# Whole float32 weights for the first two of twelve token blocks, and the second weight set decoded from block 5

## The chip, the cores and the metric

The kernel runs on one core of a Trainium2 chip. Its engines work side by side, each through its own queue in order: PE (TensorE, matrix products), DVE (VectorE), ACT (ScalarE), POOL (GpSimd) and SP, which here issues the DMAs. The metric is the time of one execution in microseconds; lower is better.

## The reference, cut to what matters

```python
# q, k, v, a_re, a_im: (4, 8, 768, 48); complex decay per step and channel, capped at 0.999
for t in range(S):
    S_re, S_im = a * S (complex product) + outer(k[t], v[t]) on the real part
    y[t] = q[t] @ S_re
x = y as (3072, 384)
gate = 1 / (1 + exp(-(x @ w_gate)))            # w_gate, w_val: 384 x 1536
x2 = (gate * (x @ w_val)) @ w_out              # w_out: 1536 x 384
h = x2 @ w_in                                  # 384 x 2048
out = (h - tanh(h)) @ w_out2                   # 2048 x 384
```

The kernel gets its weights as words of 64 bits (double precision) and makes float32 of them on the chip.

## The kernel before

The tokens are cut into 24 chunks of 128 for the recurrence ("attention") and into 12 blocks of 256 (two chunks) for the first feed-forward, called moe1. Its hidden width of 1536 is 12 slices f of 128 columns. For each block j and slice f there is one **step**, (j,f): `gv` forms the gate and value sums in PSUM from the block's x and the slice's two weight tiles; `gate` takes a tanh on ACT and forms g on DVE; `split` cuts g into a high part (ACT cast, float32r) and a low part (DVE subtraction); `outp`, three steps later (LAG1), adds g times the third weight tile to the block's output. The second feed-forward runs after all of this, in pieces of 512 tokens, on w2.

A product of float32 precision is made of three float32r products: high x high, high x low, low x high. So x, g and each weight exist as a pair of parts, and a gv step is 2 parts x 3 x 3 = 18 matmuls of 256 columns, an output step 9.

`Decoder` turns words into weights. A *tick* handles three words in three stages: `word_sign` on ACT (scaling, and the conversion of a byte), `word_value` on DVE (shift and or; with `direct` a second operation puts in the sign, otherwise ACT makes a sign tile with one more instruction and POOL multiplies by it), then `split`: an ACT cast into the high part and a POOL subtraction into the low part. `dec1` has the 36 tiles of moe1 (part 0 gate, 1 value, 2 output); seven words, listed in SIGNED, take the way with the sign tile. `dec2` has the 32 tiles of w2, all with the sign tile; they are spilled to DRAM (`w2d`) in blocks 2 to 10 and loaded back in block 11. `ring1` gives six raw buffers for the first 22 words and three for the others.

The order of steps is `order`: five steps of block 0, then steps of blocks 1 and 0 by turns, so that both use a slice soon after it is decoded, then the blocks 2 to 11 one after another. Attention for later chunks is set between the steps by due times. Within that, a scheduler fixes each engine's queue with its own estimates; SP's order is as written. PSUM holds two or three gv tiles, so a late gate holds up PE.

## Time and profile before

| | |
|---|---|
| three runs, median | 1139.35 us (1138.7 to 1139.69) |
| the profiled execution: time, span | 1139.4 us, 1137.6 us |
| PE, DVE, ACT, POOL busy, share of the span | 90%, 79%, 76%, 20% |
| gv matmuls (L735): count, busy | 2592, 348.2 us |
| output matmuls of moe1 (L769): count, busy | 1296, 187.2 us |
| matmuls of the second feed-forward (L898, L924), busy | 216.0 and 216.6 us |
| mean granted TensorE clock | 0.974 of 2.4 GHz |

A step of moe1 on blocks 2 to 11 shows as 18 + 9 matmuls and a few of attention between. The first feed-forward begins at about 79 us and ends at about 730. Busy times on PE overlap, since matmuls are pipelined: the pitch from one start to the next says more than a duration. The *gate* of a step is its DVE instruction L744 (g from th and gv).

### The profile page before, as it was taken

Reading aid. Unit: us, or ns where it says so; the run is one execution under the profiler, and the core shown is the slowest. Engines: PE = TensorE matmul, PEld = TensorE weight load, DVE = VectorE, ACT = ScalarE, POOL = GpSimd, SP = SyncE. Lnnn points to the kernel's source line nnn. Section 1 sums busy time; section 2 is a strip of 40 time slices with the busy share of each in tenths; the row PEclk is TensorE's granted clock in tenths of the full one; section 3 lists DMA queues with packets and bytes.
Section 4 is the critical chain, followed back from the end, with each engine's and each line's share of the span. In section 5 each row is a group of like instructions: output and inputs, shape, how many; then the busy total and the mean of one; then the engine's idle time right before and its main releaser. Section 6 shows DMA issues by size and latency. Waiting matters only on the chain.

```text
span 1137.6 us, 21667 instructions
## 1 busy us (share of the span) xinstructions
PE 1028.8 (90%) x8498; PEld 964.8 (85%) x8498; DVE 900.1 (79%) x1432; ACT 860.8 (76%) x1903; POOL 224.6 (20%) x182
## 2 busy tenths in 40 slices
PE   0348399999999999998999999999999999999996
PEld 0237399999999999988999999999989989999996
DVE  6999997879888988887978833487878778787875
ACT  8878796989888898877898783566767666676764
POOL 4554651131312232222323200000000000000000
PEclk9869799999999999999999999999999999999999
DMA  6223351223324424242333445700101010010000
GB/s 198 100 100 99 127 156 47 83 91 115 101 87 156 139 92 143 73 142 73 114 101 115 133 136 205 276 31 1 56 1 56 1 36 21 1 56 1 28 1 31
DMA packets 36400, 100.20 MB, mean 88 GB/s; under 512 B 4128, under 2 KB 7200, under 8 KB 36288
## 3 DMA queue, kind: packets, MB, share of 16 engines
q1 hardware_dynamic: 36288, 98.71, 26.4%
q8 instruction: 69, 1.13, 0.4%
q14 instruction: 43, 0.35, 0.1%
HBM read 76.68 MB, written 22.02 MB: 87 GB/s over the span
## 4 chain that ended last, share of the span: by engine, by line
PE 62%; DVE 14%; ACT 12%; issue 5%; DMA 3%; POOL 2%; SPq 0%; DVEq 0%; ACTq 0%; POOLq 0%
PE h L898 18%; PE o L924 17%; PE gv L735 14%; PE acc L769 7%; PE xps L604 2%; PE sc L569 2%; DMA raw<-in_w_dram 2%; DMA ri<-in_ri_dram 1%; ACT raw L68 1%; ACT raw L66 1%; DVE suf L519 1%; DVE sg L74 1%; PE gps L639 1%; POOL sg L84 1%; DVE B L532 1%
## 5 line engine op out<-in xcount | busy, mean ns | idle before, releaser
L735 PE MATMUL gv<-x,whl 128*128 128x256 f32 x2592 | 348.2, 289 | 29.6 <-DVE g L744 17.2
L735 PEld LDWEIGHTS gv<-x,whl 128*128 128x128 f32 x2592 | 327.5, 195 | 36.0 <-DVE g L744 18.3
L924 PE MATMUL o<-whl,gh 128*128 128x384 f32 x1152 | 216.6, 337 | 0.6 <-ACT gh L910 0.6
L898 PE MATMUL h<-x2h,whl 128*128 128x512 f32 x864 | 216.0, 394 | 0.0
L924 PEld LDWEIGHTS o<-whl,gh 128*128 128x128 f32 x1152 | 203.6, 188 | 9.3 <-ACT gh L910 0.9
L769 PE MATMUL acc<-gh,whl 128*128 128x256 f32 x1296 | 187.2, 288 | 3.1 <-ACT x L773 2.0
L898 PEld LDWEIGHTS h<-x2h,whl 128*128 128x128 f32 x864 | 160.9, 188 | 29.9
L769 PEld LDWEIGHTS acc<-gh,whl 128*128 128x128 f32 x1296 | 165.7, 191 | 7.8 <-ACT x L773 2.6
L91 ACT ACTIVATE s<-h 128x512 f32<-128x512 f32 x96 | 57.7, 601 | 111.3 <-PE h L898 111.3
L751 DVE TENSOR_TENSOR gh<-g,gh 128x256 fp32r<-128x256 f32 x144 | 76.6, 535 | 33.6 <-ACT gh L750 32.9
L911 DVE TENSOR_TENSOR gh<-g,gh 128x512 fp32r<-128x512 f32 x96 | 66.3, 690 | 42.0 <-ACT gh L910 41.3
L569 PE MATMUL sc<-qs,ks 112*128 112x128 f32 x384 | 56.7, 290 | 45.5 <-ACT qs L547 44.1
L99 DVE TENSOR_TENSOR th<-h,th 128x512 f32<-128x512 f32 x96 | 66.4, 692 | 31.5 <-ACT th L97 30.7
L569 PEld LDWEIGHTS sc<-qs,ks 112*128 112x128 f32 x384 | 51.3, 204 | 46.3 <-issue 34.2
L744 DVE SCALAR_TENSOR_TENSOR g<-th,gv 128x256 f32<-128x256 f32 x144 | 59.4, 413 | 36.7 <-ACT th L742 35.8
L750 ACT CAST gh<-g 128x256 fp32r<-128x256 f32 x144 | 57.8, 401 | 31.9 <-DVE g L744 31.3
L84 POOL TENSOR_TENSOR sg<-raw,sg 128x384 f32<-128x384 f32 x39 | 49.1, 1260 | 150.4 <-DVE raw L81 137.2
L100 DVE COPY_PREDICATED g<-mk,th 128x512 f32<-128x512 int32 x96 | 72.5, 755 | 1.0
L742 ACT ACTIVATE th<-gv 128x256 f32<-128x256 f32 x144 | 53.7, 374 | 25.6 <-PE gv L735 25.3
L910 ACT CAST gh<-g 128x512 fp32r<-128x512 f32 x96 | 59.3, 617 | 12.6 <-DVE g L100 12.3
L93 DVE SCALAR_TENSOR_TENSOR g<-g,s 128x512 f32<-128x512 f32 x96 | 65.5, 682 | 3.3 <-ACT g L92 3.3
L94 DVE TENSOR_TENSOR g<-g,h 128x512 f32<-128x512 f32 x96 | 65.0, 678 | 3.8 <-DVE g L93 0.9
(130 smaller groups left out, 1650.8 us busy)
## 6 DMA issues: line engine op xcount, KB each, us to landing
raw<-in_w_dram SPq DMA_DIRECT2D x68, 384.0 KB, 4.7
ri<-in_ri_dram SPq DMA_DIRECT2D x30, 448.0 KB, 4.3
w2d<-raw SPq DMA_DIRECT2D x32, 384.0 KB, 4.6
whl<-w2d SPq DMA_DIRECT2D x32, 384.0 KB, 5.0
qk<-in_qk_dram SPq DMA_DIRECT2D x24, 448.0 KB, 5.0
v<-in_vv_dram SPq DMA_DIRECT2D x24, 320.0 KB, 3.2
x2d<-x SPq DMA_DIRECT2D x12, 384.0 KB, 2.3
x2r<-x2d SPq DMA_DIRECT2D x12, 384.0 KB, 3.8
```

Source lines behind the costliest of these rows:

```text
L84: nc.gpsimd.tensor_tensor(w, raw[:, :, 0].bitcast(F32), sg, ALU.mult)
L93: nc.vector.scalar_tensor_tensor(g, g, TC * TB, s, ALU.add, ALU.mult)
L94: nc.vector.tensor_tensor(g, g, ps, ALU.mult)
L99: nc.vector.tensor_tensor(th, ps, th, ALU.subtract)
L100: nc.vector.copy_predicated(g, mk.bitcast(I32), th)
L569: nc.tensor.matmul(sc[:, i], ks[:, h // 2, h % 2], qs[:, h // 2, h % 2])
L735: nc.tensor.matmul(ps[:, part], w[:, wi, cs], x[:, xi, kt], start=(k == 0), stop=(k == 8))
L751: nc.vector.tensor_tensor(gh[:, 1], g, gh[:, 0].bitcast(F32), ALU.subtract)
L769: nc.tensor.matmul(o, w[:, wi, cs], gh[:, gi], start=(f == 0 and k == 0 and (m == 0 or m == 2 and not half)), stop=(f == NF1 - 1 and k == ...
L898: nc.tensor.matmul(ps.rearrange("p (z c) -> p z c", z=2), w[:, wi, cs], x[:, xi, :, kt], start=(k == 0), stop=(k == 8))
L911: nc.vector.tensor_tensor(gh[:, 1], g, gh[:, 0].bitcast(F32), ALU.subtract)
L924: nc.tensor.matmul(a[t], gh[:, gi, cs], w[:, wi], start=(f == 0 and k == 0), stop=(f == NF2 - 1 and k == 2), skip_group_check=True)
```

## The change

In blocks 0 and 1 (`WHOLE_GV`, `WHOLE_OUT`) the products are taken as single float32 matmuls of the whole weight, the whole x and the whole g. The decoder therefore keeps the whole float32 tiles (`F`) first; `part` makes the high and low parts of a tile later, on ACT and POOL: parts 0 and 1 of slice f after the gv step (1,f), part 2 after the output step (1,f). The whole tiles lie in slots that later hold other tiles' parts (`SLOT`, `whole_tile`), and all 36 words go through six raw buffers. For blocks 0 and 1 the low parts of x and g, and the cast of g, are gone. All words, those of w2 too, take the sign on DVE (`direct`): ACT has two instructions for a word in place of three, DVE two in place of one, POOL none in place of one. The w2 words are decoded in blocks 5 to 10 instead of 2 to 10.

```diff
-SIGNED = (6, 7, 8, 9, 10, 11, 16)
+WHOLE_GV, WHOLE_OUT = 2, 2
-SPILL_FROM, SPILL_TO = 2, 11
+SPILL_FROM, SPILL_TO = 5, 11
...
-            if 0 <= k - 2 < self.n:
+            if self.spill is not None and 0 <= k - 2 < self.n:
                 self.split(k - 2)
             if 0 <= k - 1 < self.n:
-                word_value(nc, self.raw[k - 1], self.sg[k - 1], self.sg[k - 1], self.direct(k - 1))
+                self.value(k - 1)
...
-                word_sign(nc, self.raw[k], self.sg[k], self.direct(k))
+                word_sign(nc, self.raw[k], None, True)
...
+        def value(self, s):
+            if self.spill is not None:
+                word_value(nc, self.raw[s], None, self.sg[s], True)
+                return
+            f, p = s // self.nparts, s % self.nparts
+            self.F[f, p] = whole_tile(f, p)
+            word_value(nc, self.raw[s], None, self.F[f, p], True)
+
+        def part(self, f, p):
+            w = self.F.pop((f, p))
+            hl = wp.tile([128, 2, 384], F32R, tag=f"w{SLOT[f, p]}", name="whl")
+            nc.scalar.copy(hl[:, 0], w)
+            self.low[(f * self.nparts + p) % len(self.low)].tensor_tensor(hl[:, 1], w, hl[:, 0].bitcast(F32), ALU.subtract)
+            self.W[f, p] = hl
...
+        SLOT[f, 2] = 30 + f if f < 6 else 12 + f
...
+        k, half = (24 + f, p) if p < 2 else (18 + f // 2, f % 2)
...
+            if j < WHOLE_GV:
+                nc.scalar.copy(hi.bitcast(F32), x)
+                return
...
-            w = dec1.W[f, part]
+            w = dec1.F[f, part] if j < WHOLE_GV else dec1.W[f, part]
...
+                if j < WHOLE_GV:
+                    nc.tensor.matmul(ps[:, part], w[:, cs], x[:, 0, kt].bitcast(F32),
+                                     start=(kt == 0), stop=(kt == 2))
+                    continue
...
+        if order[n][0] < WHOLE_OUT:
+            gtil[n] = m1g.tile([128, 2, N1], F32R, tag="gh", name="gh")
+            g = gtil[n][:, 0].bitcast(F32)
+            nc.vector.scalar_tensor_tensor(g, th, 1.0, ps[:, 1], ALU.add, ALU.mult)
+            return
...
+            if j < WHOLE_OUT:
+                nc.tensor.matmul(o, w[:, cs], gh[:, 0].bitcast(F32),
+                                 start=(f == 0 and (m == 0 or m == 2 and not half)),
+                                 stop=(f == NF1 - 1), skip_group_check=True)
+                continue
...
             gv(n)
+            if j == WHOLE_GV - 1:
+                dec1.part(f, 0)
+                dec1.part(f, 1)
...
                 outp(n - LAG1)
+                jo, fo = order[n - LAG1]
+                if jo == WHOLE_OUT - 1:
+                    dec1.part(fo, 2)
...
-        dec2 = Decoder(w2i, NF2, 2, ring0, lambda s: 2, (nc.gpsimd,), lambda s: False, w2d)
+        dec2 = Decoder(w2i, NF2, 2, ring0, lambda s: 2, (nc.gpsimd,), w2d)
```

The queues move with it. **PE**, among the alternating steps of blocks 1 and 0. Before, steps (1,4) and (0,9), then two output steps (x_835 is block 1's x, x_377 block 0's; the number behind x is a count of instructions):

```order
L735 MATMUL gv_1537<-x_835,whl_884 128x256 x9
L735 MATMUL gv_1537<-x_835,whl_977 128x256 x9
L735 MATMUL gv_1602<-x_377,whl_1487 128x256 x9
L735 MATMUL gv_1602<-x_377,whl_1572 128x256 x9
L769 MATMUL acc2_1298<-gh_1516,whl_874 128x256 x6
L769 MATMUL acc1_936<-gh_1516,whl_874 128x256 x3
L769 MATMUL acc0_935<-gh_1556,whl_1477 128x256 x6
L769 MATMUL acc1_936<-gh_1556,whl_1477 128x256 x3
```

After, steps (1,6) and (0,11) and two output steps (x_745 is block 1's x, x_358 block 0's; whole2 is a pair of whole tiles, and one row counts both parts):

```order
L763 MATMUL gv_1342<-x_745,whole2_981 128x256 x6
L763 MATMUL gv_1396<-x_358,whole2_1299 128x256 x6
L808 MATMUL acc2_1058<-gh_1287,whole2_854 128x256 x2
L808 MATMUL acc1_813<-gh_1287,whole2_854 128x256
L808 MATMUL acc0_812<-gh_1324,whole2_1294 128x256 x2
L808 MATMUL acc1_813<-gh_1324,whole2_1294 128x256
```

A gv step has 6 products for 18, an output step 3 for 9; a product counts once here.

**POOL**, around the work for chunk 4's ks and qs (L546 and L548 before, L571 and L573 after). Before (L84 is the sign multiplication, L312 a low part of a weight):

```order
L84 TENSOR_TENSOR sg_872<-raw_871,sg_872 128x384
L312 TENSOR_TENSOR whl_1153<-sg_882,whl_1153 128x384
L312 TENSOR_TENSOR whl_1146<-sg_872,whl_1146 128x384
L312 TENSOR_TENSOR whl_1160<-sg_892,whl_1160 128x384
L312 TENSOR_TENSOR whl_1244<-sg_985,whl_1244 128x384
L312 TENSOR_TENSOR whl_1254<-sg_996,whl_1254 128x384
L546 TENSOR_TENSOR ks_121<-qk_918,ri_703 112x4x128
L546 TENSOR_TENSOR qs_120<-qk_918,ri_703 112x4x128
L548 TENSOR_TENSOR qs_120<-qk_918,ri_703 48x4x128
L312 TENSOR_TENSOR whl_1264<-sg_1006,whl_1264 128x384
L312 TENSOR_TENSOR whl_1360<-sg_1252,whl_1360 128x384
```

After (L317 is a low part, L561 and L562 scale k and q):

```order
L561 TENSOR_TENSOR qk_626<-qk_626,suf_113 112x512
L562 TENSOR_TENSOR qk_626<-qk_626,B_631 112x512
L573 TENSOR_TENSOR ks_121<-qk_626,cosb_114 48x4x128
L571 TENSOR_TENSOR ks_121<-qk_626,ri_399 112x4x128
L571 TENSOR_TENSOR qs_120<-qk_626,ri_399 112x4x128
L577 TENSOR_TENSOR qs_120<-qk_626,cosb_114 48x4x128
L317 TENSOR_TENSOR whl_1276<-whole2_861,whl_1276 128x384
L571 TENSOR_TENSOR ks_121<-qk_795,ri_628 112x4x128
L571 TENSOR_TENSOR qs_120<-qk_795,ri_628 112x4x128
L573 TENSOR_TENSOR qs_120<-qk_795,ri_628 48x4x128
L317 TENSOR_TENSOR whl_1569<-whole2_1178,whl_1569 128x384
```

Five of the six weight instructions ahead of chunk 4's products have left that place; the low parts follow later in the queue.

**DVE**, ahead of the gate of step (1,0). Before (L74 and L77 are the two operations of a word, L744 a gate):

```order
L77 SCALAR_TENSOR_TENSOR sg_1006<-raw_1005,sg_1006 128x384
L74 SCALAR_TENSOR_TENSOR sg_1252<-raw_1251 128x384
L77 SCALAR_TENSOR_TENSOR sg_1252<-raw_1251,sg_1252 128x384
L74 SCALAR_TENSOR_TENSOR sg_1262<-raw_1261 128x384
L77 SCALAR_TENSOR_TENSOR sg_1262<-raw_1261,sg_1262 128x384
L463 TENSOR_TENSOR ri_920<-ri_920,carry_119 112x4
L464 SCALAR_TENSOR_TENSOR ri_920<-keep_110,ri_920 112x512
L548 TENSOR_TENSOR ks_121<-qk_918,ri_703 48x4x128
L74 SCALAR_TENSOR_TENSOR sg_1272<-raw_1271 128x384
L77 SCALAR_TENSOR_TENSOR sg_1272<-raw_1271,sg_1272 128x384
L744 SCALAR_TENSOR_TENSOR g_1144<-th_1142,gv_1104 128x256
L744 SCALAR_TENSOR_TENSOR g_1203<-th_1201,gv_1167 128x256
```

After (L778 is the gate):

```order
L74 SCALAR_TENSOR_TENSOR whole2_981<-raw_852 128x384
L461 SCALAR_TENSOR_TENSOR ri_797<-thB_956,ri_797 112x512
L77 SCALAR_TENSOR_TENSOR whole2_981<-raw_852,whole2_981 128x384
L74 SCALAR_TENSOR_TENSOR whole2_981<-raw_859 128x384
L471 TENSOR_TENSOR ri_797<-thA_955,thC_957 112x512
L77 SCALAR_TENSOR_TENSOR whole2_981<-raw_859,whole2_981 128x384
L778 SCALAR_TENSOR_TENSOR gh_967<-th_965,gv_942 128x256
L74 SCALAR_TENSOR_TENSOR whole2_1035<-raw_866 128x384
L488 TENSOR_TENSOR ri_797<-ri_797,carry_119 112x4
L77 SCALAR_TENSOR_TENSOR whole2_1035<-raw_866,whole2_1035 128x384
```

The gate of (1,0) stands behind 20 decoded words where it stood behind 25, and ahead of part of chunk 5's preparation.

## Rows read from the trace of the kernel before

**Rows 1.** The page: engine totals (busy us, share of the span, instructions).

```profile
PE 1028.8 (90%) x8498; PEld 964.8 (85%) x8498; DVE 900.1 (79%) x1432; ACT 860.8 (76%) x1903; POOL 224.6 (20%) x182
```

**Rows 2.** Busy by stretch: length; PE, PEld, DVE, ACT, POOL; clock; DMA share; GB/s.

```profile
8.00:167.60 159.60, 81.64 (x831) 74.24 (x832) 146.71 (x203) 135.24 (x295) 84.86 (x58) 0.84 0.37 123
167.60:219.70 52.10, 51.91 (x508) 50.32 (x507) 42.03 (x73) 40.44 (x96) 11.39 (x8) 1.00 0.25 76
...
125.00:150.00 25.00, 11.44 (x72) 11.03 (x73) 24.67 (x31) 19.47 (x43) 15.55 (x12) 0.70 0.28 81
```

**Rows 3.** Timeline of DVE, three gates (start, duration, line, tiles, form).

```profile
141.92 0.74 DVE L744 SCALAR_TENSOR_TENSOR g<-th,gv 128x256 f32<-128x256 f32 x2
...
167.23 0.41 DVE L744 SCALAR_TENSOR_TENSOR g<-th,gv 128x256 f32<-128x256 f32 x1
...
219.68 0.41 DVE L744 SCALAR_TENSOR_TENSOR g<-th,gv 128x256 f32<-128x256 f32 x1
```

**Rows 4.** Instructions of lines L735 and L569: count, ns min/median/max, first and last start.

```profile
L735 PE MATMUL gv<-x,whl x2592: 274/283/583, 79.2 to 721.7; 128*128 128x256 f32 x200
...
L569 PE MATMUL sc<-qs,ks x384: 273/275/580, 34.2 to 671.8; 112*128 112x128 f32 x192
```

**Rows 5.** Timeline of PE: unbroken runs of one line, their start and length.

```profile
170.01 4.48 PE L735 MATMUL gv<-x,whl 128*128 128x256 f32 x36
...
201.74 1.05 PE L569 MATMUL sc<-qs,ks 112*128 112x128 f32 x8
...
833.89 2.25 PE L898 MATMUL h<-x2h,whl 128*128 128x512 f32 x9
```

**Rows 6.** Lines of DVE: count, ns min/median/max (512 elements, scan, 384, 256).

```profile
L546 DVE TENSOR_TENSOR ks<-qk,ri x20: 673/676/1754, 29.7 to 650.8; 112x512 f32<-112x512 f32 x20
...
L464 DVE TENSOR_TENSOR_SCAN ri<-keep,ri x24: 1203/1224/2942, 9.0 to 621.0; 112x512 f32<-112x512 uint8 x24
...
L77 DVE SCALAR_TENSOR_TENSOR sg<-raw,sg x29: 527/557/2450, 13.9 to 175.0; 128x384 int32<-128x384 int32 x29
...
L744 DVE SCALAR_TENSOR_TENSOR g<-th,gv x144: 386/414/423, 90.4 to 722.5; 128x256 f32<-128x256 f32 x144
```

**Rows 7.** Timelines of DVE and POOL near 135 us, and two lines of POOL.

```profile
134.84 2.45 DVE L77 SCALAR_TENSOR_TENSOR sg<-raw,sg 128x384 int32<-128x384 int32 x1
...
135.88 3.20 POOL L312 TENSOR_TENSOR whl<-sg,whl 128x384 fp32r<-128x384 f32 x3
...
L312 POOL TENSOR_TENSOR whl<-sg,whl x35: 984/1325/3498, 20.7 to 176.2; 128x384 fp32r<-128x384 f32 x35
...
L84 POOL TENSOR_TENSOR sg<-raw,sg x39: 1007/1034/3125, 35.2 to 656.5; 128x384 f32<-128x384 f32 x39
```

**Rows 8.** Two lines of ACT: the sign tile and the cast of a weight.

```profile
L65 ACT ACTIVATE sg<-raw x39: 532/552/567, 22.6 to 654.3; 128x384 f32<-128x384 f32 x39
...
L310 ACT CAST whl<-sg x36: 492/500/517, 17.0 to 175.7; 128x384 fp32r<-128x384 f32 x36
```

**Rows 9.** Busy by stretch in blocks 3 to 10 (columns as in rows 2).

```profile
255.00:300.00 45.00, 44.12 (x494) 42.35 (x490) 39.79 (x66) 39.07 (x97) 10.97 (x9) 1.00 0.41 136
300.00:343.00 43.00, 40.10 (x466) 38.00 (x465) 37.22 (x64) 38.06 (x92) 9.58 (x8) 1.00 0.21 67
...
430.00:475.00 45.00, 43.62 (x498) 41.79 (x496) 37.65 (x65) 38.54 (x92) 12.69 (x9) 1.00 0.33 108
475.00:520.00 45.00, 42.29 (x457) 40.64 (x461) 35.62 (x59) 36.77 (x92) 12.30 (x9) 1.00 0.36 118
520.00:570.00 50.00, 45.04 (x409) 43.30 (x402) 43.10 (x67) 39.70 (x95) 15.73 (x12) 0.97 0.33 106
```

**Rows 10.** Timelines of ACT and PE near 305 us (in brackets: idle before, and its releaser).

```profile
304.17 0.54 ACT L68 ACTIVATE raw<-raw 128x384 int32<-128x384 uint8 x1
...
305.21 0.51 ACT L582 COPY kt<-ktp 128x448 f32<-128x448 f32 x1
305.78 0.67 PE L639 MATMUL gps<-v,kt 128*64 128x48 f32 x16 [1.47 <-ACT kt L582]
```

More of the change, by code (lines that the diff above doesn't have):

```diff
@@ L276, with __init__ @@
     class Decoder:
-        def __init__(self, src, nf, nparts, ring, depth, low, direct, spill=None):
+        def __init__(self, src, nf, nparts, ring, depth, low, spill=None):
             self.src, self.nparts, self.n, self.ring, self.depth, self.low = src, nparts, nf * nparts, ring, depth, low
-            self.direct, self.spill = direct, spill
-            self.W, self.raw, self.sg = {}, {}, {}
+            self.spill = spill
+            self.W, self.F, self.raw, self.sg = {}, {}, {}, {}
             self.loaded = self.tick_no = 0
@@ L293, in tick @@
             self.tick_no += 1
-            if 0 <= k - 2 < self.n:
+            if self.spill is not None and 0 <= k - 2 < self.n:
                 self.split(k - 2)
             if 0 <= k - 1 < self.n:
-                word_value(nc, self.raw[k - 1], self.sg[k - 1], self.sg[k - 1], self.direct(k - 1))
+                self.value(k - 1)
             self.load(k + 1)
             if k < self.n:
-                word_sign(nc, self.raw[k], self.sg[k], self.direct(k))
+                word_sign(nc, self.raw[k], None, True)
             while self.loaded < self.n and self.loaded - self.depth(self.loaded) <= k - 2 and self.loaded <= k + 4:
                 self.load(self.loaded + 1)
+        def value(self, s):
[11 more added lines that the diff above has]
+            self.W[f, p] = hl
         def split(self, s):
             w = self.sg.pop(s)
-            if self.spill is None:
-                hl = wp.tile([128, 2, 384], F32R, tag=f"w{s}", name="whl")
-            else:
-                hl = self.raw[s].rearrange("p c two -> p (c two)").rearrange("p (two c) -> p two c", two=2).bitcast(F32R)
+            hl = self.raw[s].rearrange("p c two -> p (c two)").rearrange("p (two c) -> p two c", two=2).bitcast(F32R)
             nc.scalar.copy(hl[:, 0], w)
@@ L313, in split @@
             self.W[s // self.nparts, s % self.nparts] = hl
-            if self.spill is not None:
-                nc.sync.dma_start(out=self.spill[s], in_=hl.bitcast(F32))
+            nc.sync.dma_start(out=self.spill[s], in_=hl.bitcast(F32))
         def ready(self, s):
-            while self.tick_no < min(s, self.n) + 2:
+            while self.tick_no < min(s, self.n) + 1:
                 self.tick()
@@ L323, in ring0, with whole_tile @@
                 stg.tile([128, 384], F32, tag="sg", name="sg"))
-    def ring1(s):
-        if s < 22:
-            r = wp.tile([128, 384, 2], I32, tag=f"w{24 + 2 * (s % 6)}", name="raw")
-            g = wp.tile([128, 384], F32, tag=f"w{25 + 2 * (s % 6)}", name="sg")
-            return r, g
-        return ring0(s)
-    dec1 = Decoder(w1i, NF1, 3, ring1, lambda s: 6 if s < 22 else 3, [nc.vector if s in LOW_V else nc.gpsimd for s in range(36)], lambda s: s not in SIGNED)
+    SLOT = {}
+    for f in range(NF1):
+        for p in range(2):
+            n = 2 * f + p
+            SLOT[f, p] = n if n < 18 else n + 6
+        SLOT[f, 2] = 30 + f if f < 6 else 12 + f
+    halves = {}
+    def whole_tile(f, p):
+        if (f, p) == (NF1 - 1, 2):
+            return stg.tile([128, 384], F32, tag="last", name="wlast", bufs=1)
+        k, half = (24 + f, p) if p < 2 else (18 + f // 2, f % 2)
+        if half == 0:
+            halves[k] = wp.tile([128, 2, 384], F32, tag=f"w{k}", name="whole2")
+        return halves[k][:, half]
+    def ring1(s):
+        return wp.tile([128, 384, 2], I32, tag=f"w{12 + s % 6}", name="raw"), None
+    dec1 = Decoder(w1i, NF1, 3, ring1, lambda s: 6, [nc.vector if s in LOW_V else nc.gpsimd for s in range(36)])
     mask = ap1.tile([128, 128], BF16, name="mask")
@@ L747, in split @@
     def split(n):
+        if order[n][0] < WHOLE_OUT:
+            return
         g = gtil[n]
@@ L763, in outp @@
         a0, a1, half = acc[j]
-        w = dec1.W[f, 2]
+        w = dec1.F[f, 2] if j < WHOLE_OUT else dec1.W[f, 2]
         for m in range(3):
@@ L858, in load_w2 @@
                 s = len(W2)
-                hl = wp.tile([128, 2, 384], F32R, tag=f"w{s}", name="whl")
+                hl = wp.tile([128, 2, 384], F32R, tag=f"w{SLOT[s // 3, s % 3]}", name="whl")
                 nc.sync.dma_start(out=hl.bitcast(F32), in_=w2d[s])
```

## The prediction

> **What bounds the kernel now.** I read the engine totals first, then the busy times by stretch, then the moments of the gates. Over the whole span PE is busy 90% and no other engine above 79% [rows 1], but that mean hides two regimes. Between 8 and 167.6 us PE is busy for 81.6 of 159.6 us, while DVE is busy for 146.7 and ACT for 135.2; from 167.6 to 219.7 PE is busy for 51.9 of 52.1 us [rows 2]. The border is a gate of block 1. The gates of (1,0) and (0,5) run together at 141.92, the gate of (1,3) at 167.23, that of (2,0) at 219.68 [rows 3]. So up to about 167.6 DVE sets the time (decoding words, preparing attention, gating), and from there on PE does, apart from short gaps in later blocks. Whatever the change takes from DVE counts before that border; whatever it adds to PE counts behind it, and the two must be set against each other.
>
> **PE: fewer but dearer products.** A step of blocks 0 and 1 was 18 (gv) + 9 (output) matmuls of 256 columns in float32r. It becomes 6 + 3 products in float32. Attention shows what those cost: `scores` writes 192 products of 128 columns and the trace has 384 instructions, two for each, and each lasts as long (275 ns) as a 256-column float32r matmul (283 ns) [rows 4]. So a float32 product takes two instructions, each as long as twice its columns. By pitch: 36 float32r matmuls in 4.48 us are (4.48 - 0.283) / 35 = 0.120 us each; eight instructions of `sc` in 1.05 us are (1.05 - 0.275) / 7 = 0.111 us [rows 4, 5]. With 256 columns an instruction should take nearly twice that, 0.217 us. The bounds: 0.232, the pitch of a 512-column float32r matmul (9 in 2.25 us, 0.395 long), and 0.120 if the doubling should not hold (a 256-column pitch). A gv step then goes from 18 x 0.120 = 2.16 to 12 x 0.217 = 2.61 us (+0.45), an output step from 1.08 to 6 x 0.217 = 1.30 (+0.22). From the gate of (1,3) to that of (2,0) stand 12 gv and 13 output steps, where PE has no slack: 12 x 0.45 + 13 x 0.22 = **+8.3 us**, and the two outputs of block 1 that are left after it give **+0.4**. Ahead of the border the same dearness falls on a PE that idles half the time; its cover is DVE's own length. If that cover goes, see the second rival.
>
> **DVE up to the gate of (1,3).** The instructions ahead of it in both orders, counted by size: 512 elements 66 before, 70 after; 384 elements 70 and 75; 256 elements 23 and 12; scans 18 and 18; the small ones alike. The 11 gh subtractions and the 4 low parts of x go; against them stand 70 decode operations for 61 (the seven signed words took one DVE operation, now two) and four attention operations that the order brings forward. At undisturbed durations (0.675, 0.545, 0.41, 1.21 us; 0.14 to 0.34 for 26 small ones) [rows 6] that is 119.5 us before and 120.4 after: **+0.9**, so counted alone the change gives DVE nothing.
>
> What it gives is POOL's absence. DVE was busy for 146.7 us with 119.5 us of work: 27.2 us are stretch. An L77 of median 0.56 took 2.45 us while POOL ran three subtractions from 135.88 on [rows 6, 7]. Ahead of that gate POOL has 58 products before and 37 after: 15 low parts of weights move behind it and seven sign multiplications vanish. Per POOL instruction the stretch was 27.2 / 58 = 0.47 us, so 21 fewer give **-9.9 us**. Bounds: nothing, if the stretch sits on attention's products, which stay; and -21, if each stops DVE for its whole undisturbed 1.0 us [rows 7].
>
> The Trainium skill (SBUF — State Buffer, Who interferes with whom) says that a DVE instruction with two SBUF inputs and a GpSimd instruction that reads SBUF exclude each other for a whole instruction. The long L77 looks like that; the mean of 0.47 says that only about half of POOL's time met a DVE that wanted the port. By the rule in full the first rival below follows.
>
> ACT loses work there as well: seven signs of 0.55, 15 casts of 0.50 [rows 8] and 11 gh casts of about 0.4 us, some 15 us against two more word operations. ACT was busy for 135 of 160 us and DVE idle for 12.9; I leave that idle time as it is, since the slower gv steps lengthen the same waits (plus or minus 4 for the range).
>
> So the gate of (1,3) moves from 167.2 by -9.9 + 0.9 = -9.0 us, and (2,0) by -9.0 + 8.3 = -0.7: the first two blocks are a draw. The casts and low parts that move behind the border (19 of 36) have room: in that stretch ACT was busy for 40.4 and POOL for 11.4 of 52.1 us [rows 2], and 19 x 1.3 us on POOL and 19 x 0.5 on ACT [rows 7, 8] fit. Only the part-2 tiles are made late; they wait for the last readers of their slots and are first wanted three steps into block 2.
>
> **Blocks 2 to 4 lose the decoding of w2.** In them PE idles for 0.9 us (255 to 300) and 2.9 us (300 to 343) [rows 9]. One of the gaps shows why: kt is copied at 305.21, behind a byte conversion of w2 in ACT's queue, and gps waited 1.47 us for it [rows 10]. Without such words ahead of the copies I take **-3.5** of 3.8.
>
> **Blocks 5 to 10 get it all.** 32 words in six blocks instead of nine: 5.3 instead of 3.6 a block. A word costs ACT three operations for four (16 a block for 14) and DVE two for one (10.7 for 3.6, or 3.9 us a block at 0.545); POOL has one for two. PE idles for 1.4, 2.7 and 5.0 us in three of these blocks [rows 9]. Scaled with ACT's operations, 9.1 x 16 / 14 adds **+1.2**. Bounds: -5 (the POOL multiplication leaves the chain from word to cast, and half the idle time goes), +10 (DVE, busy for 79 to 86% there, comes to 88 to 95%, and the gaps double). SP's queue is passed by nothing: loads, spills and x2d stand in the same sequence, w2's later.
>
> **The sum.** -9.0 + 8.3 + 0.4 - 3.5 + 1.2 = -2.6 us. The profiled execution took 1139.4 us, its span 1137.6, and it agrees with the median of 1139.35, so the forecast is **1136.8 us**. A measurement of this kernel can tell about 0.2% (2.3 us) from no change, so even my own sum stands near that edge: between about 1132 and 1142.
>
> **Rivals.** *POOL's lock in full (faster).* Each of 21 POOL instructions frees 1.0 us of DVE instead of 0.47: 11 us more, **1126 us**. For it speaks the 2.45 us of L77; against it, that POOL itself was stretched (median 1.33 for a least time of 0.98) and that ACT is nearly as full. This is also the time by the skill's rule.
>
> *PE too cold ahead of the border (slower).* Between the gates of (1,0) and (1,3) PE now has seven gv and five output steps, 7 x 2.61 + 5 x 1.30 = 24.8 us at full clock, in some 35 us of DVE's time (31 us of undisturbed work and its stretch). The granted clock was 0.70 between 125 and 150 us [rows 2], and an instruction at the lower level lasts twice as long (580 for 275 ns [rows 4]). If more than 10 of those 25 us run at 1.2 GHz, PE and not DVE sets the gate of (1,3); with nine tenths of them at that level it is 24.8 x 1.9 = 47 us against 35, 12 us later: **1149 us**. For it: PE stops and starts there. Against it: it is fuller than before, and at 167.6 to 219.7 the clock was whole.
>
> *Late blocks choke (slower).* DVE at 88 to 95% delays gates and kt, and PE's gaps in blocks 5 to 10 double: +9 on my sum, **1146 us**. It decides when DVE's busy share there passes what the gates can wait for; with 39 of 45 us busy (255 to 300) PE lost 0.9 us, so it need not.
>
> *Float32 doesn't double at 256 columns.* Then 0.120 a piece: a gv step falls to 1.44 us, and the stretch to (2,0) by 12 x 0.72 + 13 x 0.36 = 13.3 instead of rising by 8.3: about **1115 us**. The equal durations of 128 and 256 columns speak against it.
>
> *The split work isn't moved at all.* The order hoists the first 11 low parts into the early POOL queue anyway; that is counted in the 37. If the stretch is owed to these and to attention, the -9.9 is near zero: **1147 us**; I count that with the slower cases.
>
> **Chances.** My sum 0.44 (inside it: faster 0.21, same 0.18, slower 0.05); full lock 0.22; cold PE or no relief 0.17; late blocks 0.12 (one in four of it still within 0.2%); no doubling 0.05. Faster 0.48, same 0.21, slower 0.31. The range reaches to the full lock below and to the cold PE above, 1126 to 1149.
>
> **What would show it.** Right: gv instructions of blocks 0 and 1 twelve to a step at 0.21 to 0.23 us; the gate of (1,3) near 158; the gate of (2,0) within a few us of 219; L77 near 0.6 us in the mean; no gap of PE in blocks 2 to 4. Wrong: gate (1,3) after 165 (no relief, or PE cold: then the clock of 125 to 160 tells which), or PE idle over 15 us in blocks 5 to 10.

## The result, and the profile after

The changed kernel took **1145.99 us** (median of five; the kernel before 1139.35): a ratio of 1.0057, 95% interval 1.0042 to 1.0073. The forecast was 1136.8 with 1126 to 1149; the time lies in the range, the direction is wrong. The profiled execution took 1146.69 us, its span 1145.0.

The moments of the gates tell where it went (us; L778 is the gate of blocks 0 and 1 after the change, L781 that of the others; [rows 3] has those of before):

| gate of | before | after | moved | predicted |
|---|---|---|---|---|
| (1,0) | 141.92 | 127.15 | -14.8 | |
| (1,3) | 167.23 | 166.37 | -0.9 | -9.0 |
| (2,0) | 219.68 | 223.41 | +3.7 | -0.7 |
| (5,0) | 375.52 | 376.20 | +0.7 | -3.8 |
| (11,0) | 687.01 | 695.19 | +8.2 | -2.6 |

The DVE timeline of the changed kernel (start, duration, line, operation) has the three gates of the first half:

```profile
127.15 0.41 DVE L778 SCALAR_TENSOR_TENSOR gh<-th,gv 128x256 f32<-128x256 f32 x1
...
166.37 0.40 DVE L778 SCALAR_TENSOR_TENSOR gh<-th,gv 128x256 f32<-128x256 f32 x1
...
223.41 0.41 DVE L781 SCALAR_TENSOR_TENSOR g<-th,gv 128x256 f32<-128x256 f32 x1
```

The page's first line on the engines of the changed kernel, and PE's row with two of the dearer gv steps (start, duration, instructions, idle before them):

```profile
PE 1048.6 (92%) x8282; PEld 969.7 (85%) x8282; DVE 892.2 (78%) x1443; ACT 836.1 (73%) x1840; POOL 179.3 (16%) x143
```

```profile
204.84 5.45 PE L763 MATMUL gv<-x,whole 128*128 128x256 f32 x24 [0.56 <-DVE gh L778]
```

PE has 2% more busy time with fewer instructions; DVE's share is about what it was in [rows 1].

And the busy times by stretch (columns as in [rows 2]), up to the gate of (1,3), from there to (2,0), and from 125 to 150:

```profile
8.00:166.40 158.40, 91.03 (x784) 76.11 (x784) 143.39 (x199) 125.67 (x271) 66.67 (x40) 0.89 0.39 129
166.40:223.40 57.00, 56.01 (x323) 48.02 (x324) 36.72 (x56) 40.89 (x96) 19.82 (x18) 0.95 0.17 52
125.00:150.00 25.00, 21.82 (x130) 18.09 (x129) 24.74 (x42) 24.87 (x54) 7.85 (x5) 1.00 0.60 188
```

DVE (third) is still what is full ahead of the border. POOL (fifth) has 40 instructions for 58, DVE has lost only 3.3 us of busy time. So the step (1,0) came 14.8 us earlier, and then almost all of it was lost within the next 39 us. The same view between the gates of (1,0) and (1,3), first before the change, then after it:

```profile
142.00:167.60 25.60, 24.68 (x212) 23.08 (x213) 24.34 (x45) 23.62 (x55) 12.04 (x8) 0.91 0.47 136
```

```profile
127.20:166.40 39.20, 30.73 (x222) 25.41 (x222) 38.62 (x57) 33.14 (x73) 17.16 (x12) 0.99 0.46 143
```

More than half of the 13.9 us is order and no loss: DVE is full in both, and 12 more of its instructions stand between the two gates (57 for 45), operations of the decoding. At undisturbed durations there are 8.9 us more work between the gates, and about as much less ahead of (1,0). The rest is DVE instructions that last longer than they need to, and one of them stands out. DVE's and POOL's timelines of the changed kernel around it:

```profile
156.98 0.55 DVE L74 SCALAR_TENSOR_TENSOR whole<-raw 128x384 int32<-128x384 int32 x1
157.44 6.53 DVE L571 TENSOR_TENSOR ks<-qk,ri 112x512 f32<-112x512 f32 x1
163.90 1.47 DVE L573 TENSOR_TENSOR ks<-qk,cosb 48x512 f32<-48x512 f32 x1
```

```profile
147.14 3.82 POOL L317 TENSOR_TENSOR whl<-whole,whl 128x384 fp32r<-128x384 f32 x2 [13.07 <-ACT whl L316]
156.48 2.18 POOL L562 TENSOR_TENSOR qk<-qk,B 112x512 f32<-112x512 f32 x1 [5.51 <-DMA qk<-in_qk_dram]
158.62 6.21 POOL L317 TENSOR_TENSOR whl<-whole,whl 128x384 fp32r<-128x384 f32 x6
```

The product ks lasts 6.53 us; its median over 20 chunks is 0.676. POOL's queue is in order: L562, an attention product of chunk 5, waited 5.51 us for its qk from DRAM, and behind it six low parts of weights had become ready. When qk came, all seven ran without a pause, the six in 6.21 us (1.04 each, so POOL itself was not slowed), and DVE stood still.

### The profile page after: what moved, and what is told of

It is laid out like the page before. It is cut to its first block, busy times and chain, and to the rows that moved or that the text cites. A ratio compares the mean times of both kernels' runs of the same rounds, so it can differ in the third digit from the quotient of the medians.

```text
span 1145.0 us, 21185 instructions
## 1 busy us (share of the span) xinstructions
PE 1048.6 (92%) x8282; PEld 969.7 (85%) x8282; DVE 892.2 (78%) x1443; ACT 836.1 (73%) x1840; POOL 179.3 (16%) x143
## 4 chain that ended last, share of the span: by engine, by line
PE 65%; ACT 14%; DVE 10%; DMA 6%; issue 3%; SPq 0%; POOL 0%; ACTq 0%; DVEq 0%; POOLq 0%
PE h L948 18%; PE o L974 17%; PE gv L767 14%; PE acc L813 7%; DMA raw<-in_w_dram 3%; DMA ri<-in_ri_dram 3%; PE xps L629 2%; PE gv L763 2%; PE sc L594 2%; ACT raw L66 2%; ACT raw L68 2%; PE gps L667 1%; PE acc L808 1%; PE ktp L606 1%; DVE whole L74 1%
## 5 line engine op out<-in xcount | busy, mean ns | idle before, releaser
L767 PE MATMUL gv<-x,whl 128*128 128x256 f32 x2160 | 286.4, 286 | 2.4 <-ACT x L654 1.8
L767 PEld LDWEIGHTS gv<-x,whl 128*128 128x128 f32 x2160 | 268.9, 192 | 7.0 <-issue 2.8
L813 PE MATMUL acc<-gh,whl 128*128 128x256 f32 x1080 | 158.7, 291 | 0.4 <-DVE gh L790 0.4
L813 PEld LDWEIGHTS acc<-gh,whl 128*128 128x128 f32 x1080 | 140.3, 194 | 4.0 <-issue 1.0
L763 PE MATMUL gv<-x,whole 128*128 128x256 f32 x288 | 71.9, 405 | 21.3 <-DVE gh L778 21.3
L790 DVE TENSOR_TENSOR gh<-g,gh 128x256 fp32r<-128x256 f32 x120 | 65.0, 543 | 25.9 <-ACT gh L789 25.0
L763 PEld LDWEIGHTS gv<-x,whole 128*128 128x128 f32 x288 | 56.6, 202 | 32.5 <-DVE gh L778 24.0
L781 DVE SCALAR_TENSOR_TENSOR g<-th,gv 128x256 f32<-128x256 f32 x120 | 49.4, 413 | 35.2 <-ACT th L774 34.3
L789 ACT CAST gh<-g 128x256 fp32r<-128x256 f32 x120 | 47.9, 401 | 27.1 <-DVE g L781 26.8
```

The lines of the kernel that those rows point to most:

```text
L763: nc.tensor.matmul(ps[:, part], w[:, cs], x[:, 0, kt].bitcast(F32), start=(kt == 0), stop=(kt == 2))
L767: nc.tensor.matmul(ps[:, part], w[:, wi, cs], x[:, xi, kt], start=(k == 0), stop=(k == 8))
L790: nc.vector.tensor_tensor(gh[:, 1], g, gh[:, 0].bitcast(F32), ALU.subtract)
L813: nc.tensor.matmul(o, w[:, wi, cs], gh[:, gi], start=(f == 0 and k == 0 and (m == 0 or m == 2 and not half)), stop=(f == NF1 - 1 and k == ...
```

## Experiments on the first half: POOL's low parts

The names e1 to e22 are those of the runs. Each "Measured" gives the median time, its ratio to the kernel before, run again beside it, and the 95% interval of that ratio.

The theory (D): DVE stops while POOL subtracts, and the changed order lets subtractions pile up behind a waiting product. The rival: DVE is full by its own work, and the burst only concentrates what is lost anyway. The edits, each on the changed kernel unless it says otherwise:

```diff
 e4_after_qk_dve          (chunk 5's product on DVE)
-... (3, 4, 5), (10,))
+... (3, 4, 5), ())
 e7_after_nolow           (no low part of a moe1 weight is formed; two lines like the second)
-            self.low[...].tensor_tensor(hl[:, 1], w, hl[:, 0].bitcast(F32), ALU.subtract)
-  nc.tensor.matmul(..., w[:, wi, cs], ...)
+  nc.tensor.matmul(..., w[:, 0, cs], ...)
 e12_after_low_dve        (twelve low parts on DVE; e17: the same in the kernel before)
-LOW_V = (0,)
+LOW_V = (0, 18, 19, 21, 22, 24, 25, 27, 28, 30, 31, 33, 34)
 e16_low_dve_all          (those of all 24 gate and value tiles)
+LOW_V = tuple(s for s in range(36) if s % 3 < 2)
```

**One product moved.** 

> The changed kernel with one attention product (chunk 5, q by its magnitude, L562) on DVE in place of POOL. In the changed kernel this product stood at the head of POOL's queue, waited 5.5 us for its data, and six low parts of weights piled up behind it; DVE's ks product of chunk 5 then lasted 6.53 us for 0.68 while the six ran. Theory D (that burst locked DVE out and is why the gate of (1,3) came at 166.4): without the jam the low parts run one by one, ks takes 0.7 to 2 us, the gate of (1,3) comes at 161 to 164, that of (2,0) at 218 to 221, the time falls by 2 to 5 us. Rival (DVE is full anyway, the burst only concentrates what is lost one by one otherwise): gate of (1,3) at 165 to 167, the time within 1 us.

Measured: 1140.12 us, 1.0005 [0.9996, 1.0015], that is 5.9 us less than the changed kernel; gate of (1,3) at 162.4, of (2,0) at 218.0. DVE's timeline has no stop any more, but shares of one:

```profile
157.70 1.49 DVE L571 TENSOR_TENSOR ks<-qk,ri 112x512 f32<-112x512 f32 x1
159.11 1.49 DVE L573 TENSOR_TENSOR ks<-qk,cosb 48x512 f32<-48x512 f32 x1
160.52 1.47 DVE L573 TENSOR_TENSOR qs<-qk,cosb 48x512 f32<-48x512 f32 x1
```

On POOL, seven subtractions ran meanwhile:

```profile
152.95 11.64 POOL L317 TENSOR_TENSOR whl<-whole,whl 128x384 fp32r<-128x384 f32 x7 [1.95 <-ACT whl L316]
```

The two engines took turns: each of these DVE instructions lasts some 0.8 us longer than undisturbed. So the jam was worth 4.0 us at the gate of (1,3) and 5.4 at that of (2,0), and the subtractions cost DVE time even without it.

**The subtractions left out.** 

> The changed kernel without the low parts of moe1's weights: the 35 POOL subtractions (L317) and the one on DVE are left out, and the products that took the low part take the high part instead, so the same number of products is computed, with values that are less exact. It prices everything that these subtractions cost DVE. Theory D (DVE stands still while POOL subtracts, ahead of the gate of (1,3)): that gate at 157 to 160, the price of the subtractions 6 to 9 us there; gate of (2,0) at 213 to 216; time 1135 to 1139. Rival (DVE is full by its own work): gate at 164 to 167, time 1144 to 1147.

Measured: 1133.43 us, 0.9939 [0.9925, 0.9953]; gate of (1,3) at 152.1, 14.3 us earlier than in the changed kernel, more than theory D named; (2,0) at 212.8. The stretch between the two is of use for another step: PE has no idle moment in it, and it holds nearly the work of the one of before: 14 gv steps (12 of them whole) for 13.4, 13.7 output steps for 14.6, 24 scores in both, and 84 instructions of attention's next product (L628, L604 before) for 98.

```profile
152.10:212.80 60.70, 60.70 (x387) 52.42 (x387) 29.05 (x49) 36.04 (x84) 5.09 (x4) 1.00 0.15 49
```

60.7 us against 52.45 before is +8.25, and +8.3 was predicted for the dearer float32 products. The size is confirmed; that it fits to a tenth is luck, since the two stretches don't hold quite the same work.

**The subtractions moved to DVE.** 

> The changed kernel with twelve low parts of weights (gate and value tiles of slices 6 to 11) subtracted on DVE instead of POOL; four of them stand ahead of the gate of (1,3) in DVE's queue (4 x 0.55 = 2.2 us), and nine POOL subtractions go from there. Theory D: each POOL subtraction costs DVE its whole 1.0 us there, so the gate of (1,3) comes 6 to 8 us earlier for 2.2 us of work: 159 to 163; gate of (2,0) at 215 to 220; time 1138 to 1142. Rival (only the jam behind L562 cost something, a lone subtraction is nearly free): gate at 162 to 165, time 1140 to 1143. Rival (DVE is full by its own work): gate at 168, time 1147.

> The changed kernel with the low parts of all 24 gate and value tiles on DVE, those of slices 0 to 5 too. Theory D: a POOL subtraction costs a full DVE 0.7 to 1.0 us, on DVE it costs 0.55, so the dozen early ones give a little: gate of (1,0) at 122 to 126, gate of (1,3) at 158 to 161, time 1134 to 1137. Rival: the early ones fell into DVE's idle moments and now cost 0.55 each: gate of (1,0) at 129 to 133, of (1,3) at 164 to 168, time 1139 to 1145.

Measured: with twelve 1136.46 us, 0.9975 [0.9958, 0.9992], gates at 161.6 and 215.1; with 24, 1132.00 us, 0.9931 [0.9915, 0.9947], gates at 153.9 and 210.2. The second is faster than the kernel before by 0.7%. Up to the gate of (1,3) it shows:

```profile
8.00:153.90 145.90, 94.06 (x790) 78.68 (x790) 133.95 (x213) 124.52 (x269) 35.41 (x21) 0.94 0.44 140
```

The second's time and its gates of (1,0), at 120.7, and (1,3) come earlier than theory D had named. POOL has its 21 attention products left up to there. That allows a price for each kind of POOL instruction, if the stretch of DVE is taken row by row: the duration of each DVE instruction up to the gate of (1,3), less the median of its operation and shape where POOL is idle. (The difference of DVE's busy time and a sum of durations, as in the prediction, is too small: DVE's rows overlap by about 0.08 us, as 157.70, 1.49 and 159.11 above do, and busy time counts the overlap once. Up to that gate this makes 11.7 us before the change.)

| kernel | POOL instructions | of these attention | stretch of DVE, us | for one |
|---|---|---|---|---|
| before | 58 | 20 | 38.5 | 0.66 |
| after | 40 | 21 | 35.0 | 0.88 |
| e4 | 39 | 20 | 31.8 | 0.82 |
| e7 | 21 | 21 | 17.4 | 0.83 |
| e16 | 21 | 21 | 19.1 | 0.91 |

An attention product costs DVE 0.83 to 0.91 us where it is alone on POOL (e7, e16). With these, the 19 low parts of the changed kernel cost 15.9 to 17.6 us, **0.84 to 0.93 us each**, nearly the 1.0 that one lasts on POOL; by the same split, low parts and sign multiplications cost about 0.55 before the change. The price of a POOL instruction is no constant; it went up as the queue got shorter. The jam is a part of that (31.8 us without it, in e4); what makes the rest of the rise isn't shown. Up to the gate of (1,0) the stretch fell from 34.8 to 24.5 us, by as much as was forecast up to (1,3); between the two it grew from 3.7 to 10.5.

**The same in the kernel before.** 

> The kernel before with the same twelve low parts on DVE: does the remedy belong to the change, or would it have helped before as well? Theory D: in the kernel before, POOL's low parts come one to three at a time and stretch DVE by about 0.5 us each, as much as they cost on DVE, so little is won: gate of (1,3) at 165 to 168, time 1138 to 1141. Rival: 1 us each as in the burst: gate of (1,3) at 161 to 164, time 1134 to 1137.

Measured: gates at 163.4 and 216.7, 3.9 and 3.0 us earlier, but a time of 1138.92 us, 0.9991 [0.9980, 1.0001]. The gate agrees with the rival, the time with theory D. The gates are those of one execution, the profiled one, which took 1137.48 us: in it 2.0 us of the gain still stand at the gate of (11,0) and 1.9 at the end. The median of twelve is 1.4 us above it, so how much of the 3 us is lasting can't be told. In any case the same edit gained 9.5 us on the changed kernel (e12) and at most 2.3 us here.

**The rest on DVE.** With w2 in blocks 2 to 10 (below) and the twelve output tiles on DVE as well (`LOW_V = tuple(range(36))`): 

> The version with w2 in blocks 2 to 10 and the low parts of the 24 gate and value tiles on DVE (1129.0), now with the 12 output tiles' low parts on DVE too; these are made between about 170 and 227 us, where PE sets the time. If POOL's subtractions cost only where DVE is full: 1128 to 1130.5, gate of (2,0) at 210 to 212. If they cost everywhere: 1124 to 1127.

Measured: 1131.26 us, 0.9919 [0.9900, 0.9938], gate of (2,0) at 210.9: no gain over the 0.9904 and the 211.0 without them (e18, below). In a stretch where PE sets the time, moving the subtractions brought nothing that could be measured; the time lies above both expectations, the gate in the first.

## Experiments on the second half: where w2 is decoded

In the later blocks, the same stretches as in [rows 9] show PE (first) full where w2's decoding has gone, and short of time where it has come:

```profile
300.00:343.00 43.00, 43.00 (x491) 40.91 (x490) 33.13 (x62) 34.52 (x84) 2.72 (x2) 1.00 0.12 40
...
475.00:520.00 45.00, 43.72 (x482) 42.61 (x481) 41.47 (x69) 38.48 (x95) 11.77 (x9) 1.00 0.41 131
520.00:570.00 50.00, 46.69 (x408) 44.51 (x408) 44.60 (x74) 41.39 (x101) 10.21 (x8) 0.97 0.42 141
570.00:612.00 42.00, 39.85 (x465) 37.97 (x464) 38.04 (x68) 36.05 (x91) 7.00 (x6) 1.00 0.46 142
612.00:655.00 43.00, 40.38 (x406) 39.23 (x405) 36.59 (x60) 31.69 (x78) 14.52 (x10) 0.96 0.32 105
```

The last two stretches in the kernel before:

```profile
570.00:612.00 42.00, 41.27 (x480) 39.72 (x479) 35.31 (x65) 36.16 (x91) 7.97 (x7) 1.00 0.37 120
612.00:655.00 43.00, 42.98 (x488) 41.68 (x486) 34.13 (x58) 33.76 (x81) 14.75 (x12) 1.00 0.36 119
```

From 475 to 570 us PE idles less than before (1.3 and 3.3 us for 2.7 and 5.0), although DVE is at 92 and 89%; from 570 to 655 it idles for 4.8 us where the kernel before idled for 0.75. Between the gates of (5,0) and (8,0) the two kernels differ by 0.3 us (159.4 for 159.0), between (8,0) and (11,0) by 7.2 (159.6 for 152.4).

Theory A: the denser decoding of blocks 5 to 10 costs what was lost between 376 and 695 us. Rivals: the loss is that of the first blocks alone (B), or DVE's second operation per word is the trouble (C). The edits:

```diff
 e1, on the changed kernel; e18: the same with e16's edit; e14: with e12's; e9: with e4's
-SPILL_FROM, SPILL_TO = 5, 11
+SPILL_FROM, SPILL_TO = 2, 11
 e22, on the changed kernel; e20: the same with e16's edit
+SPILL_FROM, SPILL_TO = 2, 8
 e2, on the kernel before; e13: the same with e6's edit
-SPILL_FROM, SPILL_TO = 2, 11
+SPILL_FROM, SPILL_TO = 5, 11
 e6, on the kernel before (sign of w2 on DVE)
-dec2 = Decoder(..., lambda s: False, w2d)
+dec2 = Decoder(..., lambda s: True, w2d)
 e3, on the changed kernel (w2 by the sign tile); e5: with e1's edit; e19: with e16's
-word_sign(nc, self.raw[k], None, True)
+word_sign(nc, self.raw[k], self.sg[k], self.spill is None)
-word_value(nc, self.raw[s], None, self.sg[s], True)
+word_value(nc, self.raw[s], self.sg[s], self.sg[s], False)
```

> The changed kernel with one number put back: w2 is decoded in blocks 2 to 10 again (SPILL_FROM 2). Theory A (the loss is the denser decoding of w2 in blocks 5 to 10): the gate of (2,0) stays near 223, the 6.8 us lost in blocks 9 and 10 go, some 3.5 us of PE gaps come back in blocks 2 to 4; time 1139 to 1143. Rival B (the loss sits in the first two blocks, and what follows is chance): time stays at 1145 to 1147. Rival C (two DVE operations per w2 word are the trouble, wherever they stand): 1144 to 1148, with gaps spread over all blocks.

> The kernel before with one number changed: w2 decoded in blocks 5 to 10 (SPILL_FROM 5), everything else as it was, w2 words by the sign tile. Theory A (density alone costs): the gaps of blocks 2 to 4 go (-3.5) and blocks 5 to 10 lose 4 to 8: 1140 to 1144, blocks 9 and 10 longer than 52.4 and 45.2. Rival C (DVE's second operation per word is what costs, not density): 1135.5 to 1137, blocks 9 and 10 unchanged. Rival B (first blocks): like rival C.

> The changed kernel with w2's words through the sign tile and POOL's multiplication again (one DVE operation and three ACT operations per word), still in blocks 5 to 10. Theory A (density): 1144 to 1148, gaps by kt and x in blocks 9 and 10 as they are. Rival C (DVE's second operation): 1138 to 1141, blocks 9 and 10 near 52.4 and 45.2.

> The changed kernel with all of its treatment of w2 undone: blocks 2 to 10 (SPILL_FROM 2) and words through the sign tile. What is left of the change is the whole float32 weights of the first two blocks. Theory D (the first two blocks alone carry the lasting loss, through POOL's burst): gate of (2,0) at 222 to 224, the time 1142 to 1144. Theory A (late decoding carries it): 1138 to 1140.

Measured: e1 1143.18 us, 1.0038 [1.0024, 1.0052]; e2 1138.89, 0.9992 [0.9980, 1.0004]; e3 1143.53, 1.0035 [1.0022, 1.0048]; e5 1142.96, 1.0021 [1.0009, 1.0033]. Undoing either half of the edits to w2 gives back 2.5 to 2.8 us of the median, undoing both gives no more; the intervals of e1 and e3 overlap with that of the changed kernel, that of e5 does not. No theory holds alone: 2 to 3 us belong to the first blocks (e5), and on the kernel before the late decoding costs nothing (e2).

> The kernel before with both of the change's edits to w2 and none to the first two blocks: w2 in blocks 5 to 10, sign on DVE (two DVE operations per word). If the two edits cost only together (seen from the changed kernel: undoing either one gave 2.5 to 2.8 us back): 1141.5 to 1143. If they cost only in the company of the changed first blocks, by the order the scheduler then deals: 1138 to 1140.

> The kernel before with w2's sign on DVE, still in blocks 2 to 10. With six blocks it took 1139.4. If six blocks instead of nine cost 2 to 3 us whatever stands ahead: 1136.5 to 1137.5 here. If the cost comes only with the whole weights: 1139 to 1140.5.

Measured: e13 1139.41, 0.9996 [0.9987, 1.0005]; e6 1138.02, 0.9982 [0.9967, 0.9997], between its two expectations. So the edits to w2, alone on the kernel before, bring nothing (e13: -0.5 us, at best -1.5), where -2.3 us were predicted.

> Both steps that helped alone together: w2 in blocks 2 to 10, and chunk 5's product on DVE. If the two causes are apart: 1143.2 - 5.9 = 1137 to 1138.5, gate of (2,0) at 217 to 219. If the late part is chance that each order deals anew: 1138 to 1142.

> The changed kernel with the twelve low parts on DVE (1136.5 so far) and w2 decoded in blocks 2 to 10. If the 2.8 us that undoing the late decoding gave add up: 1133.5 to 1135. If it was chance of the order: 1136 to 1139.

> The changed kernel with the low parts of all 24 gate and value tiles on DVE (1132.0 so far) and w2 in blocks 2 to 10. If late, dense decoding costs in itself: 1129 to 1130.5. If the 2.8 us were chance of the order: 1131 to 1134.

> The same version (low parts on DVE, w2 in blocks 5 to 10) with w2's words through the sign tile: one DVE operation and three on ACT per word. If DVE's second operation is what costs: 1129 to 1130.5, blocks 9 and 10 shorter by 2 to 4 us. If it is the place or the density: 1131 to 1134, blocks 9 and 10 as they are (54.8 and 48.4).

> The same version with w2 as dense as in the changed kernel (six blocks) but earlier, in blocks 2 to 7. If density costs, blocks 2 to 7 pay and blocks 9 and 10 go back to 52.4 and 45.2: 1131 to 1134. If it is the place (blocks 9 and 10, where every delayed copy meets the tests of the first chunks): blocks 2 to 7 pay nothing, 1128 to 1130.

> The changed kernel with w2 in six blocks as it has it, but in blocks 2 to 7. From the gate of (2,0) to the end of the execution the changed kernel took 922.6 us (median less gate), with nine blocks 920.6. If density costs: 922 to 923.5, time 1145 to 1147. If the place (blocks 8 to 10) costs: 918 to 920, time 1141 to 1143.

Measured: e9 1140.10, 1.0009 [0.9994, 1.0023] (the two remedies together are not better than chunk 5's product alone); e14 1135.50, 0.9952 [0.9936, 0.9969]; **e18 1129.00, 0.9904 [0.9891, 0.9917], the fastest**, 1% below the kernel before; e19 1131.24, 0.9933 [0.9920, 0.9946]; e20 1131.30, 0.9935 [0.9921, 0.9949]; e22 1143.09, 1.0033 [1.0022, 1.0044].

In e20 the expectation speaks of the tests of the first chunks: range tests of the angles (L423 to L425, three ACT instructions a chunk), which for chunks 0 to 5 stand in the second half of block 10.

Single comparisons scatter by 1 to 2 us here, each edit makes the scheduler deal the order anew, and single executions lie up to 5 us from their median (one of e6 7). Taken together, by treatment of w2, from the profiled executions (means, us; in brackets the span of the group; the last two columns each give blocks 2 to 4, then blocks 5 to 10):

| w2 in | kernels | (2,0) to (5,0) | (5,0) to (11,0) | median time less gate of (2,0) | PE idle | lost by the clock |
|---|---|---|---|---|---|---|
| blocks 2 to 10 | before, e1, e5, e6, e9, e14, e17, e18, e21 | 157.7 (155.8 to 160.5) | 311.0 (307.8 to 313.6) | 919.9 (917.4 to 922.3) | 3.6, 9.5 | 0.2, 2.3 |
| blocks 5 to 10 | after, e2, e3, e4, e7, e12, e13, e16, e19 | 151.9 (149.9 to 153.2) | 318.7 (315.9 to 322.5) | 921.1 (919.5 to 922.6) | 0.1, 11.7 | 0.0, 3.2 |
| blocks 2 to 7 | e20, e22 | 160.8 | 306.2 | 919.3 | 5.2, 8.4 | 0.0, 0.9 |

(Lost by the clock is the length of a stretch times what its mean granted clock lacks of 1.00.) In the two columns of stretches the first two groups don't overlap: 5.8 us shorter without w2, 7.7 longer with all of it. But a gate is no clean border of PE's work: the second group starts 1610 PE instructions for 1629 in the first stretch and 3229 for 3199 in the second, so at 0.12 us each some 2.3 of the 5.8 and 3.6 of the 7.7 us are work that came later. PE's idle time has the rest: leaving w2 out of blocks 2 to 4 brings 3.4 us, packing it into 5 to 10 costs 2.2 and up to 0.9 by the clock. The column with the median has the sum, with what block 11 and the second feed-forward add: about +1.2, less than the kernels of one group differ among themselves. With each profiled execution's own time in place of the median it is +0.5, and seven pairs of kernels that differ in this edit alone (after and e1, e16 and e18, e12 and e14, e4 and e9, e3 and e5, e13 and e6, e2 and before) give +1.4 in the mean of their ratios, from -0.9 to +3.1. So the later decoding costs of the order of 1 us, at the edge of the scatter; e18, 3 us faster than e16, is the top of that range.

Within the blocks 2 to 10 the place of w2 mostly moves PE's idle time: idle and clock together are 15.5, 15.0 and 14.4 us in the three groups. Whether density or place makes the 1 us isn't shown. The third group is as dense as the second and no dearer than the first, which speaks against density, but it has two kernels, and the time of e20 lies in the range that was written down for a cost of density (2.0 of its 2.3 us over e18 stand at the gate of (2,0) already). e19 against e16 (0.9933 and 0.9931) says that the second DVE operation isn't it.

What the changed kernel lost in blocks 8 to 10 is a case for itself, (8,0) to (11,0). First the changed kernel, then e1 (nine blocks), then e22 (none of w2 there), with nearly as many matmuls each:

```profile
535.60:695.20 159.60, 153.36 (x1594) 147.61 (x1594) 124.44 (x220) 125.82 (x315) 30.77 (x24) 0.97 0.43 139
```

```profile
538.40:689.40 151.00, 146.98 (x1589) 142.63 (x1588) 115.46 (x208) 118.94 (x299) 22.94 (x18) 1.00 0.37 118
```

```profile
541.80:690.60 148.80, 148.11 (x1589) 143.02 (x1588) 97.90 (x188) 106.94 (x269) 10.41 (x8) 1.00 0.21 64
```

PE's idle time is 6.2, 4.0 and 0.7 us; that explains 2.2 of the 8.6 us between the first two. The clock explains more: it fell three times in the changed kernel, and not once in e1.

```profile
535.60:538.60 3.00, 3.00 (x21) 3.00 (x21) 2.73 (x6) 2.39 (x5) 1.00 (x1) 0.71 0.77 305
625.00:631.00 6.00, 5.81 (x95) 5.40 (x95) 4.35 (x8) 5.54 (x16) 2.30 (x2) 0.72 0.01 3
690.00:695.20 5.20, 5.05 (x29) 5.05 (x30) 2.76 (x7) 2.64 (x5) 0.00 (x0) 0.67 0.28 102
```

Together that is 4.3 us at full clock (3.0 x 0.29 + 6.0 x 0.28 + 5.2 x 0.33); some 2 us of the 8.6 stay unexplained. Ahead of each fall PE had waited:

```profile
532.89 0.94 PE L594 MATMUL sc<-qs,ks 112*128 112x128 f32 x6 [1.97 <-DVE qs L577]
...
625.19 0.67 PE L667 MATMUL gps<-v,kt 128*64 128x48 f32 x16 [2.11 <-ACT kt L607]
...
689.56 0.38 PE L767 MATMUL gv<-x,whl 128*128 128x256 f32 x1 [1.00 <-ACT x L654]
```

The second of them in windows:

```profile
620.00:625.00 5.00, 3.08 (x26) 2.88 (x25) 4.53 (x8) 4.97 (x10) 0.00 (x0) 1.00 0.40 123
625.00:628.00 3.00, 2.81 (x28) 2.76 (x29) 1.35 (x3) 3.00 (x9) 0.51 (x1) 0.68 0.00 0
628.00:631.00 3.00, 3.00 (x69) 2.64 (x68) 3.00 (x6) 2.54 (x8) 1.79 (x2) 0.75 0.02 5
```

Behind the wait of 2.11 us for kt the granted clock was 0.68 and 0.75 of 2.4 GHz for 6 us, so more than half of them at 1.2 GHz: up to 1.7 us lost for 2.1 of waiting. ACT was busy all the time around it; the copy of kt stood in its queue behind the angles of the next chunks, w2's words and a table load:

```profile
620.14 0.54 ACT L66 ACTIVATE raw<-raw 128x384 f32<-128x384 f32 x1
620.59 0.54 ACT L68 ACTIVATE raw<-raw 128x384 int32<-128x384 uint8 x1
...
622.27 1.28 ACT L509 ACT_TABLE_LOAD   x1
...
624.62 0.51 ACT L607 COPY kt<-ktp 128x448 f32<-128x448 f32 x1
```

In e1 the same copy came as late, with the same kinds of ACT work ahead of it, and the clock stayed whole:

```profile
626.00 0.67 PE L667 MATMUL gps<-v,kt 128*64 128x48 f32 x16 [2.02 <-ACT kt L607]
```

```profile
624.00:630.00 6.00, 4.00 (x92) 3.62 (x93) 3.85 (x9) 5.63 (x14) 1.01 (x1) 1.00 0.01 3
```

So this wait isn't the packing's doing, and not every gap has the price of a slower clock. Nor do the falls separate the groups: in blocks 8 to 10 they cost 2.4 us with w2 in blocks 5 to 10 and 1.7 with w2 in blocks 2 to 10. What decides whether the clock falls behind a gap isn't settled by these runs.

## Why the prediction was wrong, step by step

- **What bounds the kernel**: right. DVE up to the gate of (1,3), PE behind it; in the changed kernel PE waited 10.1 us for gates between 127 and 168 us.
- **The dearer products**: right. A float32 product of 256 columns is two instructions; 24 of them took 5.45 us with 0.38 for one, a pitch of (5.45 - 0.38) / 23 = 0.220 us (0.217 forecast). The +8.3 showed where PE had no gaps (e7). In the changed kernel the stretch to (2,0) grew by 4.6 only, because with a gate of (1,3) that late PE had less left to do behind it: 16 scores for 24, 11.7 output steps for 14.6. 1 us of it was idle, and the clock was 0.95 for 1.00.
- **POOL's absence, -9.9**: this is the step that failed. It priced each POOL instruction that goes at the mean of before, and took that mean as a constant. The counts were nearly right (40 for 37 after the change), the price wasn't: the stretch of DVE fell from 38.5 to 35.0 us, 3.5 us less, not 9.9, because what stayed cost 0.88 us each for 0.66; and DVE's idle time, which was left as it is, rose by 2.1. Low parts went from about 0.55 to 0.84 to 0.93. The row with the 2.45 us of L77 behind three subtractions [rows 7] already showed what a queue of ready subtractions does; I used its mean. The mean itself, 0.47, was read too low as well: it set DVE's busy time, which counts overlaps once, against a sum of durations. Read rightly, 0.66, the same step would have forecast still more gain (-13.9).
- **The two rivals there**: the lock in full was nearer to the truth about the price, with the sign against the change: it made the 19 low parts that stayed dearer. The Trainium skill (SBUF — State Buffer, Who interferes with whom) states that exclusion. The 6.53 us of ks agrees with it; the mean of 0.66 us before the change, less than the 0.98 of the shortest subtraction [rows 7], says that not every POOL instruction stopped DVE for its whole length. PE too cold did not happen: the clock from 125 to 150 us was 1.00, for 0.70 before.
- **Blocks 2 to 4, -3.5**: right. The waits for kt vanished, PE's idle time in these blocks went from 3.8 us to none in the changed kernel, and from 3.6 to 0.1 in the means over 18 kernels.
- **Blocks 5 to 10, +1.2**: mis-sized. In the means PE's idle time there rose by 2.2 us and the loss by the clock by up to 0.9; in the profile of the changed kernel by 1.4 (11.2 for 9.8) and up to 3.4 (5.1 for 1.7). The clock was no term of the sum. Between the gates the changed kernel lost 7.5 us (319.0 for 311.5), of which 19 more PE instructions are some 2.3. The rival *late blocks choke* gave 1146 us, which is the measured time; that is luck, since about half of the miss stands ahead of these blocks.
- **The sum**: of 9.2 us between forecast and median, 4.4 stood at the gate of (2,0) and 4.8 behind it. Of the 4.8, some 3.5 belong to w2 by the medians of the groups (+1.2 for the forecast -3.5 + 1.2 = -2.3); 2.0 of these show as PE's idle time and clock (-0.3 for -2.3). The rest is of the size of the scatter and stays open.
